# Retention attention with a two-of-eight router and experts: states per head, outputs on four quarter arrays, routed rows in threes, noise loaded later

## The chip, the cores and the metric

The kernel runs on one core of one Trainium2 chip. The metric is the device time of one execution in microseconds (us). A run is called slow when it is more than 1.5% above the fastest run of the same kernel; ratios use fast runs only. On one core a single run's state can't be known, so the two runs that were taken once are called "unknown" below.

The profile names the engines PE (TensorE's matmuls), PEld (its weight loads), DVE (VectorE), ACT (ScalarE), POOL (GpSimd) and SP (SyncE). A name with q behind it, such as SPq, is the part of an engine that issues DMAs.

## The reference

Attention without softmax, with a decay per head, then a noisy router that sends each row to two of eight experts:

```python
# q, k, v: (8 batches, 8 heads, 576 rows, 64); N = 4608 rows, D = 512, E = 8 experts, F = 1024
scores = (1 / sqrt(64)) * q @ k.transpose(0, 1, 3, 2)
gamma  = 1 - 2.0 ** (-5 - arange(8))
Dmat   = where(rel >= 0, gamma[:, None, None] ** rel, 0)          # rel = row - column
x      = ((scores * Dmat) @ v) -> (4608, 512)
noisy  = x @ w_gate + log1p(exp(x @ w_noise)) * noise
top2   = the two largest of noisy; weights = softmax over the two
out[row] += weight * (relu(x[row] @ w1[e]) @ w2[e])               # for both experts of the row
```

## The kernel before

The attention works in 16 units of one batch and four heads. A unit takes its 512 rows as four blocks of 128: it makes scores S within a block, a running state T (keys times values) for what lies before the block, and the output x from both. Units come in four groups of four; when a group is done, its two batches (nine columns of 128 rows) are routed while the next group is computed. The routed rows go to a buffer `xd` in DRAM, from which the experts gather them.

The states, once for each pair of heads (hp), full 128 by 128 products of which only the two diagonal blocks are kept:

```python
def states(self, u, hp):
    p = self.ps.tile([P, 4, P], F32, name="T", bufs=1)
    for c in range(2):
        for k, n in ((P, slice(2 * c + 1, 4)), (HD, slice(2 * c, 2 * c + 1))):
            for r in range(2):
                m = d["vn"][:k, r, c, hs, :]...to_broadcast([k, n.stop - n.start, P])
                nc.tensor.matmul(p[:, n, :], lhsT=d["kn"][:k, r, c, hs, :]..., rhs=m, ...)
    for h in range(2):
        s = slice(h * HD, (h + 1) * HD)
        nc.scalar.activation(T[s, :, s], p[s, :, s], Act.Copy)
```

The output, once for each half e of a block; q is a row half of the array, s a column half:

```python
def out(self, u, e):
    p = self.ps.tile([P, 2, 2, P], F32, name="x", bufs=2)
    q = slice(e * HD, (e + 1) * HD)
    for hp in range(2):
        for c in range(2):
            for r in range(2):
                for h in range(2):
                    nc.tensor.matmul(p[s, hp, c, :], lhsT=d["vn"][q, r, c, 2 * hp + h, :], rhs=d["S", hp, h][q, c, r, :], ...)
    ...  # three more matmuls of 128 by 128 per hp with the states, then VectorE's eviction to xT
```

The router's noise, loaded at the start by ScalarE's queue, and the storing of the routed rows, after all else of a route, one column of 128 rows at a time:

```python
self.rows = ctx.enter_context(tc.tile_pool(name="rtx", bufs=3))
...
for j in range(2):
    for c in range(4):
        nc.scalar.dma_start(out=self.noise[j * HD:(j + 1) * HD, :, c, :], in_=nq[:, j, :, c, :])
    nc.scalar.dma_start(out=self.noiset[j * HD:(j + 1) * HD], in_=nt[:, j])
...
for c in range(C):                                   # C = 9
    pt = ps.tile([P, DM], BF16, name="tr", bufs=2)
    ...                                              # four transposes
    xr = self.rows.tile([P, XW], F32, name="xr")
    nc.scalar.activation(xr[:, :DM // 2].bitcast(BF16), pt, Act.Copy)
    nc.gpsimd.tensor_copy(xr[:, DM // 2:], pl[:, c, :])
    nc.sync.dma_start(out=self.xd[(c0 + c) * P:(c0 + c + 1) * P, :], in_=xr)
    yield
```

A route is a generator: between two parts of a unit the loop runs it on to its next `yield`. So the number of `yield`s says over how many places of the attention a route is spread.

Of the kernel before, what the change touches and what calls it, by code (L numbers as in the profile page):

```python
# [16 lines left out]
P = 128  # L17
N = 4608
NCOL = N // P
E = 8  # L20
# [68 lines left out]
def decay_tables(nc, cp, tmp):  # L89
# [4 lines left out]
    tv = tmp.tile([P, 576], F32, name="tv")  # L94
# [21 lines left out]
class Attention:  # L116


    def __init__(self, tc, ctx, K, q, k, v):
# [11 lines left out]
        self.Tb = [self.cp.tile([P, 4, P], BF16, name=f"Tb{j}") for j in range(8)]  # L131
# [54 lines left out]
    def cast_tail(self, bp):  # L186
        nc = self.nc
        d = {}
        for n in "qk":
            t = self.bf.tile([P, DM], BF16, name=n + "t")  # L190
# [55 lines left out]
    def states(self, u, hp):  # L246
# [4 lines left out]
        p = self.ps.tile([P, 4, P], F32, name="T", bufs=1)  # L251
        hs = slice(2 * hp, 2 * hp + 2)
        first = True
        for c in range(2):

            for k, n in ((P, slice(2 * c + 1, 4)), (HD, slice(2 * c, 2 * c + 1))):
                for r in range(2):
                    m = d["vn"][:k, r, c, hs, :].rearrange("p h d -> p (h d)").unsqueeze(1).to_broadcast(
                        [k, n.stop - n.start, P])
                    nc.tensor.matmul(p[:, n, :], lhsT=d["kn"][:k, r, c, hs, :].rearrange("p h d -> p (h d)"), rhs=m,  # L260
                                     start=first, stop=(c == 1 and k == HD and r == 1), skip_group_check=True)
                    first = False
        T = self.Tb[(2 * u + hp) % 8]
        for h in range(2):
            s = slice(h * HD, (h + 1) * HD)
            nc.scalar.activation(T[s, :, s], p[s, :, s], Act.Copy)  # L266
        d["T", hp] = self.T[bp, b, 2 * hq + hp] = T

    def out(self, u, e):

        nc = self.nc
        d = self.u[u]
# [3 lines left out]
        p = self.ps.tile([P, 2, 2, P], F32, name="x", bufs=2)  # L276
        q = slice(e * HD, (e + 1) * HD)
        for hp in range(2):
            for c in range(2):
                for r in range(2):  # L280
                    for h in range(2):
                        s = slice(h * HD, (h + 1) * HD)
                        nc.tensor.matmul(p[s, hp, c, :], lhsT=d["vn"][q, r, c, 2 * hp + h, :],  # L283
                                         rhs=d["S", hp, h][q, c, r, :], start=(hp == 0 and c == 0 and r == 0),
                                         stop=False, skip_group_check=True)
        for hp in range(2):
            for c in range(2):
                j = 2 * c + e
                if j:
                    nc.tensor.matmul(p[:, hp, c, :].rearrange("p (r q) -> p r q", r=2), lhsT=d["T", hp][:, j - 1, :],  # L290
                                     rhs=d["Q"][:, hp, c, :, e, :], start=False, stop=(hp == 1 and c == 1),
                                     skip_group_check=True)
        xv = self.xT[bp][:, 2 * hq:2 * hq + 2, 4 * b:4 * b + 4, :].rearrange("p y (c e) t -> p y c e t", e=2)[:, :, :, e, :]
        gv = self.gt[:, 2 * hq:2 * hq + 2, :512].rearrange("p y (c e t) -> p y c e t", c=2, e=2)[:, :, :, e, :]
        nc.vector.tensor_tensor(xv, p, gv, Alu.mult)
        if e:
            del self.u[u]
# [28 lines left out]
class Router:  # L326
    def __init__(self, tc, ctx, K, at, wgn, moe_noise, xd, keep):
# [8 lines left out]
        nm = moe_noise.rearrange("(b s) e -> b s e", b=8)  # L336
        nq = nm[:, :512, :].rearrange("b (c q r) e -> q r b c e", q=HD, r=2)
        nt = nm[:, 512:, :].rearrange("(p b) s e -> s b p e", b=2)
        for j in range(2):
            for c in range(4):  # L340
                nc.scalar.dma_start(out=self.noise[j * HD:(j + 1) * HD, :, c, :], in_=nq[:, j, :, c, :])
            nc.scalar.dma_start(out=self.noiset[j * HD:(j + 1) * HD], in_=nt[:, j])
# [4 lines left out]
    def route(self, bp):  # L347
# [7 lines left out]
        for c in range(C):  # L355
# [3 lines left out]
            if c % 3 == 2:  # L359
                yield  # L360
# [638 lines left out]
```

## Time and profile before

| | before |
|---|---|
| timed, three runs | 698.31, 702.89, 708.54 us |
| profiled execution, span | 630.6 us |
| first scores of unit 0 | 35.05 us |
| first scores of units 5, 9, 13 | 83.40, 153.23, 215.02 us |
| end of the attention | 263.4 us |
| first expert matmul | 310.27 us |

The times of units are the starts of their first group of scores (S) on TensorE. The first expert matmul divides the kernel in two: the change touches only what lies before it.

These are the groups of the page that concern the states, the stored rows and the two matmuls of the experts. The columns are line, engine, operation, operands and count, then busy time in all and mean ns of one, then the idle time just ahead of them and what ended most of it.

```profile
L738 PE MATMUL p<-xgT,w 128*128 128x256 bf16 x1280 | 244.4, 275 | 2.4 <-DVE hT L745 0.3
L757 PE MATMUL po<-w,hT 128*128 128x512 bf16 x600 | 226.5, 381 | 6.3 <-DVE o L788 6.3
...
L260 PE MATMUL T<-vn,kn 64*128 64x128 bf16 (+2 forms) x256 | 51.7, 324 | 8.2 <-ACT Tb L266 8.2
...
L266 ACT ACTIVATE Tb<-T 64x256 bf16<-64x256 f32 x64 | 24.2, 378 | 63.1 <-PE T L260 62.7
...
L513 POOL COPY xr<-pl 128x8 f32<-128x8 f32 x36 | 9.9, 292 | 77.9 <-DMA xd<-xr 62.1
...
L512 ACT ACTIVATE xr<-tr 128x512 bf16<-128x512 bf16 x36 | 20.9, 597 | 37.0 <-DMA xd<-xr 19.9
```

Two things are to be seen. The states are the largest TensorE item of the attention (51.7 us busy), and the two engines that fill row buffers wait 62.1 and 19.9 us for stores of rows. And the experts' matmuls run almost without a gap: 2.4 and 6.3 us idle.

### The profile page before, as it was taken

The numbers are of one execution on the slowest core, as the hardware profiler recorded it, in microseconds if no ns is written. First come the engines' busy times: TensorE is split into PE (matmuls) and PEld (weight loads), VectorE is DVE, ScalarE is ACT, GpSimd is POOL, SyncE is SP. The second block draws the span as 40 slices with busy tenths as digits, with TensorE's granted clock in tenths as the row PEclk, the third lists the DMA queues.
The fourth block names the chain that finished last, engine by engine and source line by source line (L and its number), as shares of the span: only waits on it lengthen the run. The fifth ranks groups of instructions, "written<-read, shape, count | busy, mean of one in ns | idle before, by whom it ended". The sixth has DMA issues, their size and how long they took to land.

```text
span 630.6 us, 11565 instructions
## 1 busy us (share of the span) xinstructions
PE 479.9 (76%) x4329; PEld 329.6 (52%) x4369; DVE 277.4 (44%) x727; ACT 296.5 (47%) x449; POOL 313.3 (50%) x393
## 2 busy tenths in 40 slices
PE   0179985757657966604499999999896999999990
PEld 0155653534435644403366666666674666667660
DVE  0034467622782477384422244443442444444440
ACT  5164552334624540603257575666664666544430
POOL 8504324303512310012670277777777767777773
PEclk9999975565658555856599999999998999999996
DMA  9999855094915100411354676778778489666552
GB/s 196 239 267 290 189 151 118 6 219 146 266 27 102 45 2 1 135 76 63 89 160 161 216 273 211 249 231 259 251 273 278 161 287 331 194 198 213 175 190 88
DMA packets 112251, 110.76 MB, mean 176 GB/s; under 512 B 28802, under 2 KB 84611, under 8 KB 112192
## 3 DMA queue, kind: packets, MB, share of 16 engines
q1 hardware_dynamic: 86080, 76.18, 41.0%
q0 software_dynamic: 19232, 32.87, 19.4%
q10 hardware_dynamic: 6880, 0.93, 1.0%
q8 instruction: 35, 0.57, 0.4%
q14 instruction: 24, 0.20, 0.1%
HBM read 91.21 MB, written 41.83 MB: 211 GB/s over the span
## 4 chain that ended last, share of the span: by engine, by line
PE 57%; DVE 14%; DMA 10%; issue 6%; ACT 4%; POOL 4%; SPq 3%; ACTq 0%; POOLq 0%; DVEq 0%
PE p L738 20%; PE po L757 18%; PE T L260 5%; DMA xd<-xr 3%; PE x L283 3%; DMA prv<-yd,ix 2%; PE pt L722 2%; PE tr L222 2%; SPq L153 2%; PE R L498 2%; DVE olo L482 2%; DVE S L243 1%; DMA out_dram<-o,ix 1%; PE S L238 1%; DMA rawt_q<-in_q_dram 1%
## 5 line engine op out<-in xcount | busy, mean ns | idle before, releaser
L738 PE MATMUL p<-xgT,w 128*128 128x256 bf16 x1280 | 244.4, 275 | 2.4 <-DVE hT L745 0.3
L757 PE MATMUL po<-w,hT 128*128 128x512 bf16 x600 | 226.5, 381 | 6.3 <-DVE o L788 6.3
L738 PEld LDWEIGHTS <-w 128*128 128x128 bf16 x1280 | 126.4, 99 | 89.2 <-issue 8.6
L745 DVE TENSOR_SCALAR hT<-p 128x512 bf16<-128x512 f32 x80 | 55.1, 690 | 149.7 <-PE p L738 148.2
L743 ACT ACTIVATE hT<-p 128x512 bf16<-128x512 f32 x80 | 47.8, 597 | 119.3 <-PE p L738 81.4
L766 POOL DMA_INDIRECT prv<-yd,ix x70 | 71.5, 1022 | 50.5 <-DVE hT L745 27.5
L693 POOL DMA_INDIRECT xg<-xd,xi x80 | 80.7, 1009 | 27.1 <-issue 15.5
L794 POOL DMA_INDIRECT out_dram<-o,ix x70 | 71.1, 1016 | 21.4 <-issue 13.1
L243 DVE TENSOR_TENSOR S<-S,mask 128x512 bf16<-128x512 f32 x64 | 41.1, 683 | 82.2 <-PE S L238 82.2
L757 PEld LDWEIGHTS <-hT 128*128 128x128 bf16 x640 | 62.9, 98 | 8.6
L788 DVE SCALAR_TENSOR_TENSOR o<-po,f,prv 128x512 f32<-128x512 f32 x70 | 50.0, 744 | 23.1 <-DMA prv<-yd,ix 19.9
L260 PE MATMUL T<-vn,kn 64*128 64x128 bf16 (+2 forms) x256 | 51.7, 324 | 8.2 <-ACT Tb L266 8.2
L777 ACT ACTIVATE y<-po,f 128x512 f32<-128x512 f32 x80 | 50.4, 683 | 10.0 <-PE po L757 10.0
L266 ACT ACTIVATE Tb<-T 64x256 bf16<-64x256 f32 x64 | 24.2, 378 | 63.1 <-PE T L260 62.7
L178 POOL TENSOR_TENSOR vn<-raw_v,vg 128x1024 bf16<-128x1024 f32 x16 | 30.4, 1902 | 43.0 <-PE x L283 25.3
L173 POOL TENSOR_SCALAR_AFFINE_SELECT kn<-raw_k 128x512 bf16<-128x512 f32 x32 | 22.1, 716 | 58.5 <-PE T L260 37.5
L513 POOL COPY xr<-pl 128x8 f32<-128x8 f32 x36 | 9.9, 292 | 77.9 <-DMA xd<-xr 62.1
L689 ACT ACTIVATE w<-wst 128x1024 bf16<-128x1024 f32 x48 | 47.8, 1047 | 0.0
L725 ACT ACTIVATE xgT<-pt 128x1024 bf16<-128x1024 bf16 x40 | 40.7, 1017 | 10.0 <-DVE f L707 7.6
L260 PEld LDWEIGHTS <-kn 128*128 128x128 bf16 (+1 forms) x256 | 18.3, 108 | 39.9 <-issue 36.1
L222 PE MATMUL tr<-ident,qb 128*128 128x128 bf16 x128 | 15.9, 300 | 29.6 <-ACT qb L182 29.6
L512 ACT ACTIVATE xr<-tr 128x512 bf16<-128x512 bf16 x36 | 20.9, 597 | 37.0 <-DMA xd<-xr 19.9
(167 smaller groups left out, 553.4 us busy)
## 6 DMA issues: line engine op xcount, KB each, us to landing
wst<-in_moe_w_dram SPq DMA_DIRECT2D x48, 512.0 KB, 5.8
yd<-y SPq DMA_DIRECT2D x35, 512.0 KB, 3.7
raw_k<-in_k_dram SPq DMA_DIRECT2D x32, 256.0 KB, 5.7
raw_v<-in_v_dram SPq DMA_DIRECT2D x32, 256.0 KB, 5.2
raw_q<-in_q_dram SPq DMA_DIRECT2D x30, 256.0 KB, 5.4
xd<-xr SPq DMA_DIRECT2D x36, 132.0 KB, 1.7
w<-in_moe_w_dram POOLq DMA_DIRECT2D x4, 1024.0 KB
xg<-xd,xi POOLq DMA_INDIRECT x80
```

What stands on the lines that cost most here:

```text
L243: nc.vector.tensor_tensor(S, p[h], self.K["mask"].unsqueeze(1).to_broadcast([P, 2, 2, P]), Alu.mult)
L260: nc.tensor.matmul(p[:, n, :], lhsT=d["kn"][:k, r, c, hs, :].rearrange("p h d -> p (h d)"), rhs=m, start=first, stop=(c == 1 and k == HD a ...
L689: nc.scalar.activation(W[e][:, k * F:(k + 1) * F], t, Act.Copy)
L693: nc.gpsimd.indirect_dma_start(out=xgs[i % NX][:, s, :], out_offset=None, in_=xd[:, :], in_offset=IOff(ap=keep["xi"][:, 2 * i + s:2 * i + ...
L738: nc.tensor.matmul(p1[:, f2, :], lhsT=w[:, o:o + P], rhs=xgT[:, di, :], start=(di == 0), stop=(di == KD - 1))
L743: nc.scalar.activation(hT[:, 2 * fp:2 * fp + 2, :], p1, Act.Relu)
L745: V.tensor_relu(hT[:, 2 * fp:2 * fp + 2, :], p1)
L757: nc.tensor.matmul(po[s], lhsT=hT[:, fi, s * P:(s + 1) * P], rhs=w[:, o:o + DM], start=(fi == 0), stop=(fi == KF - 1))
L766: nc.gpsimd.indirect_dma_start(out=prv[i % NP][:, s, :], out_offset=None, in_=yd[:rows, :], in_offset=IOff(ap=st[i]["ix"][:, s, 1:2], axis=0),
L777: nc.scalar.activation(y[:, s, :], po[s], Act.Copy, scale=g[:, s:s + 1])
L788: V.scalar_tensor_tensor(o[:, s, :], st[i]["po"][s], st[i]["g"][:, s:s + 1], prv[i % NP][:, s, :], Alu.mult, Alu.add)
L794: ins = nc.gpsimd.indirect_dma_start(out=out[:, :], out_offset=IOff(ap=st[i]["ix"][:, s, 0:1], axis=0), in_=st[i]["o"][:, s, :], in_offset ...
```

## The change

Its intent: fewer and shorter steps for TensorE in a unit (states only for the blocks that are kept, outputs on all four quarters of the array), no wait for stores of rows (three buffers of three columns, filled early in the route), and a start that does not stand behind the noise. The diff, cut to its core:

```diff
-    def states(self, u, hp):
+    def states(self, u):
-        p = self.ps.tile([P, 4, P], F32, name="T", bufs=1)
+        p = self.ps.tile([P, 2, 4, HD], F32, name="T", bufs=1)
         for c in range(2):
             for k, n in ((P, slice(2 * c + 1, 4)), (HD, slice(2 * c, 2 * c + 1))):
                 for r in range(2):
-                    m = d["vn"][:k, r, c, hs, :]...to_broadcast([k, n.stop - n.start, P])
-                    nc.tensor.matmul(p[:, n, :], lhsT=d["kn"][:k, r, c, hs, :]..., rhs=m, ...)
+                    for hp in range(2):
+                        for h in range(2):
+                            m = d["vn"][:k, r, c, 2 * hp + h, :]...to_broadcast([k, n.stop - n.start, HD])
+                            nc.tensor.matmul(p[h * HD:(h + 1) * HD, hp, n, :], lhsT=d["kn"][:k, r, c, 2 * hp + h, :], rhs=m, ...)
         for h in range(2):
-            nc.scalar.activation(T[s, :, s], p[s, :, s], Act.Copy)
+            nc.scalar.activation(T[s, :, :, s]..., p[s]..., Act.Copy)
[...]
-    def out(self, u, e):
+    def out(self, u):
-        p = self.ps.tile([P, 2, 2, P], F32, name="x", bufs=2)
+        p = [self.ps.tile([P, 2, 2, P], F32, name="x", bufs=2) for e in range(2)]
         for hp in range(2):
             for c in range(2):
                 for r in range(2):
                     for h in range(2):
-                        nc.tensor.matmul(p[s, hp, c, :], lhsT=d["vn"][q, r, c, 2 * hp + h, :], rhs=d["S", hp, h][q, c, r, :], ...)
+                        for e in range(2):
+                            q = slice(e * HD, (e + 1) * HD)
+                            nc.tensor.matmul(p[e][s, hp, c, :], lhsT=d["vn"][q, r, c, 2 * hp + h, :], rhs=d["S", hp, h][q, c, r, :], ...)
[...]
+    def load_noise(self, j):          # called in units 1 and 2, on SyncE's queue
[...]
     def route(self, bp):
+        xr = [self.rows.tile([P, 3, XW], F32, name="xr") for j in range(3)]
+        def row(c):
+            ...                       # four transposes, then
+            nc.scalar.activation(xr[c // 3][:, c % 3, :DM // 2].bitcast(BF16), pt, Act.Copy)
+        row(0)                        # one row(c) after each of the next steps
[...]
+        for j in range(3):            # ahead of the tables olo and oh
+            nc.gpsimd.tensor_copy(xr[j][:, :, DM // 2:], pl[:, 3 * j:3 * j + 3, :])
+            nc.sync.dma_start(out=self.xd[t0:t0 + 3 * P, :]..., in_=xr[j])
-        for c in range(C):            # the loop of nine single rows at the end
-            ...
[...]
         at.load(0, (nc.scalar, nc.sync, nc.sync))
-        at.load_tail(0, (nc.scalar, nc.sync, nc.sync))
-        for u in (1, 2, 3):
+        at.load(1, (nc.scalar, nc.sync, nc.sync))
+        at.load_tail(0, (nc.sync,) * 3)
+        for u in (2, 3):
             at.load(u, (nc.sync,) * 3)
[...]
-        at.cast_tail(0)               # now at the end of unit 0
-        at.tr_tail(0)
```

"Tails" are the last 64 rows of each batch, which don't fill a block. The route's product for the ranks (line 455 after) also moved, behind the computation of the weights.

## The prediction

> **What bounds the kernel now.** I read the busy slices first, to split the span into stages; then the chain of waits in order of time, for what ends last in each; then the timeline of single stretches, for the length of one step.
>
> ```profile
> PE   0179985757657966604499999999896999999990
> DVE  0034467622782477384422244443442444444440
> PEclk9999975565658555856599999999998999999996
> DMA  9999855094915100411354676778778489666552
> ```
>
> One slice is 15.8 us. From slice 20 on (about 310 us) TensorE is nearly full: the experts, which the change does not touch. Before it lie two slices of almost no TensorE work, sixteen units of attention with routing between them, and from 263 to 310 us a trough. No engine is full there, so that part is a chain of waits. The first expert matmul starts at 310.27 us; whatever comes off before it comes off the end. The timed runs (702.89 us) are 70 us longer than the profiled execution (630.6 us of span). Nothing in the page tells where those 70 us lie; I assume that they lie in what stays.
>
> Start, from the timeline:
>
> ```profile
> 16.48 5.38 ACTq L341 DMA_DIRECT2D noise<-in_moe_noise_dram  x4
> 22.30 0.60 ACTq L342 DMA_DIRECT2D noiset<-in_moe_noise_dram  x1
> 22.94 4.40 ACTq L341 DMA_DIRECT2D noise<-in_moe_noise_dram  x4
> 28.45 1.06 ACT L182 ACTIVATE qb<-raw_q 128x1024 bf16<-128x1024 f32 x1 [15.30 <-DMA noise<-in_moe_noise_dram]
> ```
>
> ScalarE's own queue issues ten noise loads before it may cast the first q: 15.30 us idle, though both casts of k were over at 13.6 us. Unit 0 starts its scores at 35.1 us.
>
> A unit without routing, TensorE's timeline:
>
> ```profile
> 42.99 0.64 PE L238 MATMUL S<-QT,KT 64*64 64x128 bf16 x16
> 43.42 1.06 PE L283 MATMUL x<-S,vn 64*64 64x128 bf16 x16
> 44.42 0.39 PE L290 MATMUL x<-QT,Tb 128*128 128x128 bf16 x2
> ...
> 48.27 1.83 PE L260 MATMUL T<-vn,kn 128*128 128x384 bf16 x8
> 51.01 1.78 PE L260 MATMUL T<-vn,kn 128*128 128x384 bf16 x8 [0.92 <-ACT Tb L266]
> 52.72 0.64 PE L238 MATMUL S<-QT,KT 64*64 64x128 bf16 x16
> ```
>
> From S to S is one unit: 9.73 us. TensorE sets it; only the second T waits, for the eviction of the first out of the one T buffer. The same 16 matmuls of 64x64 by 128 columns take 0.43 us as S and 1.00 us as x (start to next start).
>
> A unit in which routed rows are stored, and the last route:
>
> ```profile
> 144.33 0.60 ACT L512 ACTIVATE xr<-tr 128x512 bf16<-128x512 bf16 x1 [9.24 <-DMA xd<-xr]
> 144.98 1.01 PE L222 MATMUL tr<-ident,kn 128*128 128x128 bf16 x8 [7.59 <-ACT xr L512]
> ```
>
> ```profile
> 282.62 2.46 DVE olo L482
> ...
> 289.04 2.58 PE R L498 x18
> 292.13 0.61 ACT xr L512
> 292.79 2.09 DMA xd<-xr
> ...
> 299.53 1.71 DMA xd<-xr
> 301.31 0.59 issue
> ```
>
> Three row buffers for nine rows: ScalarE waits for a store that stands in SyncE's queue behind loads, and TensorE waits for ScalarE. At the end the nine rows follow each other by themselves, after the last table is finished.
>
> **What the Trainium skill says.** "TensorE: Matmul & The Clock Gate", Part 3 (packing small matmuls): tiles of the array at different row and column positions run at once. The trace agrees: S alternates over four quarters, 27 ns a matmul; x keeps one row half and alternates two columns, 62 ns. The same page, Part 1, has a cold clock at half rate, 107 ns for 128 columns. The trace agrees in durations (8 transposes from 47.42 to 48.27 us, 106 ns each; 68 ns each from 78.04 to 78.58), though the granted clock in the page reads 9 in both. "TensorEngine Tiling (Array Packing)", Key Properties: a change of tiling mode drains the engine. The T group streams 2 x 384 + 6 x 128 columns, 1.28 us at the cold rate, and took 1.63 to 1.83, so four changes of shape may cost 0.35 us or more. "DMA: Bandwidth & Descriptors", Specifications, wants 512 bytes or more for line rate; the noise lies in pieces of 32 bytes, and its queue (q10) took 1.0% of 16 engines' span, 6.3 us, for 0.93 MB including two q loads. Agreed.
>
> **The change part by part.**
>
> *Start.* The noise goes to SyncE during units 1 and 2, unit 1 is loaded before the tails, the tail casts come after unit 0. ScalarE ends its tables at 13.1 us and can cast q then, if q has landed (loads here took 5 to 8 us). Cast 1.06, transposes 1.05, two evictions of 1.02, less overlap: scores at about 17.5 us instead of 35.1. Gain 17.6 us.
>
> *Outputs.* 32 matmuls go from 2.00 us to 32 x 27 ns = 0.87 us: 1.1 us a unit cold, 0.5 us warm.
>
> *States.* Two heads' full product, of which half was thrown away, becomes one column half per head: 8 matmuls of 192 columns and 24 of 64, run in pairs. Four pairs of 160 ns plus 12 pairs of 60 to 110 ns plus drains of 0.4 us: 2.1 us, instead of 48.27 to 52.72 = 4.45 us. Gain 2.3 us, of which 0.9 is the wait for the T buffer. ScalarE: two evictions of 512 columns at about 0.6 us (its row of 512 columns took 597 ns) for four of 378 ns, 0.3 us less.
>
> *A unit without routing:* 9.7 - 1.1 - 2.3 = 6.3 us. DMA is near: the loads run full up to 65 us, 16.2 MB in 65 us, 250 GB/s; a unit with its share of tails is 1.7 MB or 6.7 us, and the noise now adds 6 us in between. So I take 17.5 us + 4.5 (unit 0) + four steps of about 7 + 2 for tails and noise: step 5 begins at 52 us instead of 83.4. Gain 31 us, the start included.
>
> *Routing.* The steps that lay on the path go: TensorE no longer waits for the cumulated counts (2.00 us at 96.90) since that product comes after the weights; three buffers of three rows, filled during the route, replace three of one row. VectorE's work stays: per four units 16 S of 683 ns, 8 xT of 688 ns, tails about 3 us, and the route, about 15 us (150.0 us busy before 304 us, less S, xT, tails and memsets, over 4), together 34 to 37 us. By the order of VectorE's instructions the route now falls into the first three steps of each four. Step 5: about 11.8 us of VectorE; step 6: 15.2 (olo 2.5, oh 1.65 twice); steps 7 and 8 are TensorE's, 8.7 (with 18 table matmuls) and 7.6. Sum 43 us, 45 with some blocking. Before, the groups took 70 us (83.4 to 153.2), 62 us (to 215.0) and 48 us (to 263.4, its last step without a new unit). After: 45, 45 and 40. Gains 25, 17 and 8: 50 us. The attention would end at 52 + 130 = 182 us.
>
> *End.* From 263.4 to 292.4 us (the list of rows) VectorE's chain is kept; it includes 7 us of memsets. The gather began at 302.13 us because of the rows' stores; with the rows stored under olo and oh it can begin about 0.5 us after the list. Gain 9 us. Gather to first expert matmul, 8 us, stays.
>
> *Sum.* 17.6 + 13.8 (31.4 in all up to step 5) + 50 + 9 = 90 us. The profiled span becomes about 540 us; the timed median 702.9 - 90 = 613 us. I write 615.
>
> **The rivals.**
>
> *DMA becomes the bound.* Faster units demand loads faster. Sixteen units at 6.7 us, noise 6 us, four halves of expert weights of about 7 us each, stores of two routes about 4.5 us each: 150 us until unit 15 has landed. Step 14 wants it; by my sum the middle of step 14 is at about 161 us. So it only just does not bind. For it: DMA share above 1 up to 65 us. Against: it was idle at 105 to 125 and 180 to 195 us. If it bound by 20 us, 635 us.
>
> *VectorE takes the whole gain of the states.* The route is packed into fewer steps, its olo and oh stand in front of evictions of S, and TensorE waits there. For it: TensorE already waited 20.9 us for oh and 12.7 us elsewhere for VectorE's copies. Against: two whole steps of each four are free of routing. If the groups took 55, 55 and 45 us, 640 us.
>
> *Outputs and states gain nothing* because small matmuls are bound by their issue. Against: S shows 27 ns a matmul, 17 ns when warm. Then units stay at 9.7 us and only start, rows and end remain, about 45 to 50 us: 655 us.
>
> *Better than the sum:* a TensorE with fewer gaps runs warm more often (a unit at about 4 us instead of 6.3), and the 70 us of the timed runs may lie partly in the part that shrinks: 590 us.
>
> **Range and chances.** Three rivals cost 20 to 40 us and hardly all at once; one gains 25. 80% range 588 to 648 us. Even the start and the end alone, 27 us, are 3.8% of 703, and neither depends on another engine's speed beyond loads that have landed. Faster by over 2%: 0.96; within 2%: 0.03; slower: 0.01.
>
> **What would show it.** The first S at about 17 us (if q lands late, it shows as a wait on q's load). A unit of 6 to 7 us between 25 and 50 us; x on four quarters at 27 ns or less a matmul, T as one group of about 2 us without a wait in it. No wait of ScalarE on the stores of rows. S evictions late behind olo and oh in step 6. The attention's end at about 182 us, the first gather right after the list, the first expert matmul at about 220 us and 320 us of experts after it. The prediction would be wrong if the noise loads, now on SyncE in front of the loads of units 5 and 6, starved TensorE there; if 64-column states took as long as before; or if the expert stage itself became longer.

## The result, and the profile after

The changed kernel is correct and takes 628.92 us (median of four runs, 620.63 to 632.7); the kernel before took 703.41 us in the median of the four runs beside it (698.31 to 708.54). The ratio is 0.8902, with a 95% interval from 0.8785 to 0.9019: faster. A ratio here is the mean time of one kernel's fast runs over the mean of the other's fast runs of the same rounds, so it is not quite the quotient of the two medians. The profiled execution of the changed kernel spans 626.8 us.

The busy slices of the changed kernel, 15.7 us each, in tenths:

```profile
PE   0688668558763246999889889699699779889980
...
DVE  0366886896887741222334334144144224323440
...
PEclk9977657658656558899979889789889979969996
DMA  9997999996023222447646647457667764554542
```

Counted from 0, the trough before the experts now lies at slices 12 to 14, where the kernel before had it at 17 to 19. But from slice 16 on the experts show digits of 6 and 7 every few slices, which the kernel before did not show in its profile.

Two units before routing starts, TensorE's timeline of the changed kernel (start, length, engine, line, operation, then in brackets an idle time and what ended it):

```profile
28.26 0.64 PE L238 MATMUL S<-QT,KT 64*64 64x128 bf16 x16
28.68 1.07 PE L285 MATMUL x<-S,vn 64*64 64x128 bf16 x32
29.68 0.82 PE L293 MATMUL x<-QT,Tb 128*128 128x128 bf16 x6
30.30 1.06 PE L222 MATMUL tr<-ident,qb 128*128 128x128 bf16 x8
31.29 0.64 PE L238 MATMUL S<-QT,KT 64*64 64x128 bf16 x16
31.86 1.04 PE L222 MATMUL tr<-ident,kn 128*128 128x128 bf16 x8
32.83 1.25 PE L259 MATMUL T<-vn,kn 128*64 128x192 bf16 x32
34.33 0.42 PE L238 MATMUL S<-QT,KT 64*64 64x128 bf16 x16 [0.25 <-ACT KT L225]
```

From S to S it is 6.07 us, where the kernel before took 9.73. All 32 output matmuls take 1.00 us (28.68 to 29.68), as long as 16 of them took before; the states are one group of 1.25 us with nothing to wait for inside. (TensorE works at two rates in these traces: eight transposes of 128 columns in a row start about 107 ns apart at one and 56 ns apart at the other. "Cold clock" and "warm clock" below mean these two. The states and the S after them ran on the warm clock, so not all of the 3.66 us is the change.)

The unit ahead of it went less well. It starts at 17.34 us, and then TensorE stands still for the tails:

```profile
20.96 1.91 PE L259 MATMUL T<-vn,kn 128*64 128x192 bf16 x32
24.96 0.29 PE L209 MATMUL tr<-ident,qt 128*128 128x128 bf16 x1 [2.10 <-ACT qt L193]
27.40 0.29 PE L209 MATMUL tr<-ident,kt 128*128 128x128 bf16 x1 [2.15 <-POOL kt L195]
```

The end of the last route in the changed kernel:

```profile
217.45 2.56 PE L524 MATMUL R<-oh,olo 128*128 128x160 bf16 x18 [7.95 <-DVE oh L518]
...
220.79 0.24 DVE L540 SCALAR_TENSOR_TENSOR xi<-xrow,z 128x80 int32<-128x80 f32 x1
221.89 1.15 POOL L708 DMA_INDIRECT xg<-xd,xi  x1 [6.63 <-DVE cT L555]
```

The list of rows (`xi`) is written at 221.0 us and the first gather starts at 221.9; before, the list was there at 292.6 and the gather began at 302.1.

ScalarE's filling of the row buffers, whose wait for stores was 19.9 us, now waits mostly for TensorE's transposes. From the page after:

```profile
L367 ACT ACTIVATE xr<-tr 128x512 bf16<-128x512 bf16 x36 | 20.7, 595 | 15.8 <-PE tr L366 11.5
```

And the experts' two groups of matmuls, after:

```profile
L753 PE MATMUL p<-xgT,w 128*128 128x256 bf16 x1280 | 261.9, 286 | 26.3 <-issue 23.4
L772 PE MATMUL po<-w,hT 128*128 128x512 bf16 x640 | 253.7, 400 | 19.1 <-issue 14.6
```

They stood idle for 26.3 and 19.1 us, mostly for "issue": the profile shows nothing they waited for. The experts took 395.8 us (231.0 to 626.8) against 320.3 us in the profile of before. So the first expert matmul came 79.3 us earlier, the profiled execution became only 3.8 us shorter, and the timed runs 74.5 us shorter. Taken at its word, the pair of profiles would say that the change saved 79 us and lost 75 of them in the experts. The timed runs contradict that, which is what the first experiment settles.

### The profile page after: what moved, and what is told of

It reads as the page before. It is cut to its first block, busy times and chain, and to the rows that moved or that the text cites. A ratio compares the mean times of both kernels' runs of the same rounds, so it can differ in the third digit from the quotient of the medians.

```text
span 626.8 us, 11951 instructions
## 1 busy us (share of the span) xinstructions
PE 472.1 (75%) x4625; PEld 317.9 (51%) x4625; DVE 282.9 (45%) x727; ACT 291.9 (47%) x417; POOL 318.1 (51%) x365
## 4 chain that ended last, share of the span: by engine, by line
PE 59%; DVE 17%; issue 11%; DMA 4%; ACT 4%; SPq 2%; POOL 1%; another core or an unknown queue 1%; ACTq 0%; POOLq 0%; DVEq 0%
PE p L753 25%; PE po L772 23%; DVE S L243 3%; PE pt L737 2%; PE T L259 2%; DMA raw_q<-in_q_dram 2%; PE R L524 2%; DVE olo L508 2%; DVE xT L299 1%; PE tr L222 1%; DMA xg<-xd,xi 1%; DVE oh L516 1%; DVE oh L513 1%; PE S L238 1%
## 5 line engine op out<-in xcount | busy, mean ns | idle before, releaser
L753 PE MATMUL p<-xgT,w 128*128 128x256 bf16 x1280 | 261.9, 286 | 26.3 <-issue 23.4
L772 PE MATMUL po<-w,hT 128*128 128x512 bf16 x640 | 253.7, 400 | 19.1 <-issue 14.6
L753 PEld LDWEIGHTS <-w 128*128 128x128 bf16 x1280 | 129.9, 102 | 134.6 <-issue 61.1
L772 PEld LDWEIGHTS <-hT 128*128 128x128 bf16 x640 | 64.7, 101 | 33.3 <-issue 23.4
L792 ACT ACTIVATE y<-po,f 128x512 f32<-128x512 f32 x80 | 51.7, 685 | 34.8 <-remote 17.7
L243 DVE TENSOR_TENSOR S<-S,mask 128x512 bf16<-128x512 f32 x64 | 41.1, 683 | 37.7 <-PE S L238 37.7
L704 ACT ACTIVATE w<-wst 128x1024 bf16<-128x1024 f32 x48 | 47.9, 1049 | 0.0
L427 POOL TENSOR_TENSOR cum<-cum,M 128x8 bf16<-128x8 bf16 x36 | 7.2, 199 | 64.5 <-DVE d L432 62.0
L173 POOL TENSOR_SCALAR_AFFINE_SELECT kn<-raw_k 128x512 bf16<-128x512 f32 x32 | 24.0, 775 | 26.4 <-DMA raw_k<-in_k_dram 14.1
L265 ACT ACTIVATE Tb<-T 64x512 bf16<-64x512 f32 x32 | 18.8, 589 | 35.6 <-PE T L259 33.5
L737 PE MATMUL pt<-ident,xg 128*128 128x128 bf16 x320 | 26.5, 225 | 9.4 <-DMA xg<-xd,xi 7.0
L737 PEld LDWEIGHTS <-xg 128*128 128x128 bf16 x320 | 22.0, 100 | 11.8 <-DMA xg<-xd,xi 8.6
L222 PE MATMUL tr<-ident,qb 128*128 128x128 bf16 x128 | 13.7, 272 | 17.4 <-ACT qb L182 14.6
```

Of the source, the lines that this page charges most:

```text
L243: nc.vector.tensor_tensor(S, p[h], self.K["mask"].unsqueeze(1).to_broadcast([P, 2, 2, P]), Alu.mult)
L704: nc.scalar.activation(W[e][:, k * F:(k + 1) * F], t, Act.Copy)
L737: nc.tensor.transpose(pt[:, di, s * P:(s + 1) * P], xb[:, di * P:(di + 1) * P], K["ident"])
L753: nc.tensor.matmul(p1[:, f2, :], lhsT=w[:, o:o + P], rhs=xgT[:, di, :], start=(di == 0), stop=(di == KD - 1))
L772: nc.tensor.matmul(po[s], lhsT=hT[:, fi, s * P:(s + 1) * P], rhs=w[:, o:o + DM], start=(fi == 0), stop=(fi == KF - 1))
L792: nc.scalar.activation(y[:, s, :], po[s], Act.Copy, scale=g[:, s:s + 1])
```

## The experiments

All kernels but one give correct results. The table has, for each profile, the first scores of units 0, 5, 9, 13 and 15, the first expert matmul, and the rest of the span, which is the experts. All in us.

| run | unit 0 | 5 | 9 | 13 | 15 | first expert matmul | experts |
|---|---|---|---|---|---|---|---|
| before | 35.0 | 83.4 | 153.2 | 215.0 | 242.3 | 310.3 | 320.3 |
| before, again | 34.8 | 83.2 | 151.8 | 211.4 | 237.0 | 304.3 | 398.3 |
| changed | 17.3 | 56.1 | 104.0 | 152.2 | 180.6 | 231.0 | 395.8 |
| outputs by halves | 17.3 | 55.7 | 104.6 | 152.7 | 181.5 | 231.0 | 393.2 |
| old states | 17.4 | 65.2 | 121.9 | 178.9 | 210.0 | 261.6 | 397.0 |
| old start | 34.0 | 65.4 | 113.3 | 161.1 | 189.5 | 239.1 | 399.9 |
| late single rows | 17.4 | 57.4 | 123.9 | 178.2 | 204.3 | 267.3 | 401.9 |
| old route | 17.3 | 55.9 | 116.0 | 169.6 | 195.2 | 270.6 | 401.3 |
| tables made once | 17.4 | 56.3 | 103.9 | 148.7 | 174.4 | 223.8 | 396.3 |
| memsets on GpSimd | 17.4 | 56.3 | 104.0 | 151.5 | 179.9 | 224.4 | 398.6 |
| late rows in threes | 17.3 | 54.3 | 105.8 | 159.0 | 185.1 | 243.7 | 397.8 |
| tables spread | 17.3 | 56.0 | 105.6 | 155.7 | 182.0 | 236.8 | 399.9 |
| tail loads later | 17.4 | 57.0 | 105.4 | 153.6 | 181.8 | 232.6 | 402.2 |
| best | 17.3 | 54.1 | 98.8 | 148.4 | 177.2 | 218.3 | 403.3 |

One caution for reading it: the same code may differ by 4 to 6 us from one profile to the next. The last row has the changed kernel's attention, and is at unit 9 at 98.8 against 104.0 us; the two profiles of the kernel before have their first expert matmul at 310.3 and 304.3 us. Each row is one profile, so differences of a few us in this table show nothing by themselves.

### The kernel before, once more

No edit; one more profile of the kernel before.

> The kernel before, unchanged. Its timed runs took 703 us and its profile 631 us, of which the experts (from the first expert matmul at 310 us) took 320 us without gaps; the changed kernel's experts took 396 us in its profile, with TensorE idle in bursts for nothing that the profile shows. Theory: the profile of before fell into a rarer state of the expert stage; a new profile shows the first expert matmul at 310 us again, within 3 us, and about 390 us after it. Rival: the 70 us lie in attention and routing, which the profile flattered; then the first expert matmul comes near 380 us and 320 us follow.

It took 704.15 us, span 702.6, and its first expert matmul stands at 304.3 us. Its experts took 398.3 us and look like those of the changed kernel:

```profile
L738 PE MATMUL p<-xgT,w 128*128 128x256 bf16 x1280 | 260.4, 287 | 25.5 <-issue 21.1
L757 PE MATMUL po<-w,hT 128*128 128x512 bf16 x640 | 253.4, 400 | 23.8 <-issue 19.2
```

So the first profile of before caught a rare execution in which the experts ran almost without gaps. In all 13 other profiles the experts took 393 to 403 us, whichever kernel it was. The change therefore did not slow the experts, and the 70 us by which the timed runs exceed the first profile lie in the experts, as the prediction had assumed. Profile against typical profile, the change gains 73.3 us before the experts (304.3 to 231.0), which agrees with 74.5 us timed.

Where the experts lose the time can be seen in part. Counting each 32 of the first expert product's matmuls as one tile of rows, most tiles take 7.4 us from start to start in every profile, and some take 10 to 20 us: in the changed kernel the tiles 1, 9, 12, 14, 18, 23, 28 and 33 took 18.4, 15.1, 11.4, 13.0, 18.4, 17.1, 18.6 and 18.8 us, and inside them single matmuls of one accumulation start 0.5 to 2 us apart with no semaphore between them. Counted at 10 us and over, 7 to 16 of the 39 tile-to-tile times are long in these 13 profiles. They are not scattered by chance: tiles 1, 9 and 23 are long in all 13, and in the first profile of before only tile 23 is (14.6 us), so the places go with the program, though not what is lost there. I looked for a cause in the fetches of instructions (DMA queues 8 and 14). Some lie inside the long stretches of the changed kernel (at 445.8 us in the one from 444.9 to 456.3) and some of these stretches have none (239.9 to 251.3 us), so they don't explain it. What makes the tiles long was not settled.

### Outputs by halves

```diff
-        for hp in range(2):
-            for c in range(2):
-                for r in range(2):
-                    for h in range(2):
-                        for e in range(2):
+        for e in range(2):
+            for hp in range(2):
+                for c in range(2):
+                    for r in range(2):
+                        for h in range(2):
                             nc.tensor.matmul(p[e][s, hp, c, :], ...)
```

> The changed kernel, but the 32 output matmuls of a unit issued row half by row half again, so that two quarters run at a time. Theory: 32 of them take 2.0 us instead of 1.0 us at the cold rate (0.55 us more when warm), 16 units, TensorE bounds only the steps without routing: first expert matmul 6 to 14 us later than 231 us, time 1 to 2% longer. Rival (VectorE or transfers bound every step): less than 3 us.

It took 629.96 us, ratio 0.9002 (0.8947 to 0.9057), and the first expert matmul came at 231.01 us where the changed kernel has 231.00. My theory fell and the rival held: interleaving all four quarters is worth nothing on the path that these runs can show. The group itself did get longer, on the cold clock and the warm one:

```profile
29.12 1.50 PE L285 MATMUL x<-S,vn 64*64 64x128 bf16 x32
...
42.23 0.87 PE L285 MATMUL x<-S,vn 64*64 64x128 bf16 x32
```

against 1.07 and 0.62 us after the change. That is less than expected. The trace's single matmuls show two chains of eight pairs, the second of which begins at 29.55 us, when three pairs of the first have still to start (29.65 to 29.87 us). The trace doesn't name the row halves; I take the chains for them. The 0.25 to 0.43 us that remain, 4 to 7 us over 16 units, don't appear at the first expert matmul; either other engines end last in those units, or they are lost in the 4 to 6 us by which profiles differ. This run keeps both halves in one call, as the change has it; the older form with two calls at two places of the unit was not run by itself.

### Old states

```diff
-        p = self.ps.tile([P, 2, 4, HD], F32, name="T", bufs=1)      # one group of 32, per head
-        ...
+        for hp in range(2):                                          # two groups of 8, as before
+            p = self.ps.tile([P, 4, P], F32, name="T", bufs=1)
+            ...
+            for h in range(2):
+                nc.scalar.activation(T[s, hp, :, s], p[s, :, s], Act.Copy)
```

> The changed kernel with the states of before: full 128x128 products, two per unit through one T buffer, four evictions. Theory: a unit that TensorE bounds gets 2.3 to 3 us longer, a step that VectorE bounds less; over 16 units first expert matmul 20 to 35 us later, time 3 to 6% longer. Rival (hidden behind VectorE and loads): under 8 us.

It took 661.07 us, ratio 0.9418 (0.9358 to 0.9478); the first expert matmul moved by 30.6 us, to 261.6. The theory holds. Between units 5 and 9 it lost 56.7 - 47.9 = 8.8 us, and between 9 and 13 57.0 - 48.2 = 8.8 us: 2.2 us a unit in both. The lines show the wait that the change removed, here on the warm clock (the narrower products and the missing wait were not parted by a run):

```profile
42.16 1.15 PE L261 MATMUL T<-vn,kn 128*128 128x384 bf16 x8
44.22 1.13 PE L261 MATMUL T<-vn,kn 128*128 128x384 bf16 x8 [0.91 <-ACT Tb L267]
45.28 0.25 PE L319 MATMUL x<-St,vt 128*64 128x128 bf16 x2
```

### Old start

```diff
-        at.load(1, (nc.scalar, nc.sync, nc.sync))
-        at.load_tail(0, (nc.sync,) * 3)
-        for u in (2, 3):
+        at.load_tail(0, (nc.scalar, nc.sync, nc.sync))
+        for u in (1, 2, 3):
             at.load(u, (nc.sync,) * 3)
         ...
+        rt.load_noise(0)              # on ScalarE's queue again
+        rt.load_noise(1)
         ...
+        at.cast_tail(0)
+        at.tr_tail(0)
```

> The changed kernel with the start of before: noise loaded by ScalarE's queue at once, tails before unit 1 and cast before unit 0. Theory: first S near 35 us instead of 17.3; since the first units of the changed kernel wait for loads (unit 1 began at 28.3 us), the late start is partly caught up: first expert matmul 8 to 14 us later. Rival of my own prediction: the whole 17.6 us come back.

It took 640.09 us, ratio 0.9101 (0.9052 to 0.9149). Unit 0 starts 16.7 us later, unit 5 is 9.3 us later, and the first expert matmul 8.1 us; the median is 11.2 us higher. So a start that is 17 us earlier is worth half of that, or somewhat more. With the noise in front unit 0 takes 5.2 us (34.0 to 39.2) and not 10.9: the loads of units 1 to 3 have more time, and the tails are cast and transposed before unit 0 and not at its end. GpSimd's timeline of the changed kernel shows what holds the tails there:

```profile
23.04 1.27 POOL L173 TENSOR_SCALAR_AFFINE_SELECT kn<-raw_k 128x512 bf16<-128x512 f32 x2 [4.66 <-DMA raw_k<-in_k_dram]
24.88 1.90 POOL L178 TENSOR_TENSOR vn<-raw_v,vg 128x1024 bf16<-128x1024 f32 x1 [0.57 <-DMA raw_v<-in_v_dram]
26.73 0.61 POOL L195 TENSOR_SCALAR_AFFINE_SELECT kt<-rawt_k 128x512 bf16<-128x512 f32 x1
```

The cast of the tail's keys (`kt`) stands behind the casts of unit 2, and those wait for the loads of unit 2, though the tail's loads were issued before them (9.5 to 15.1 us against 15.1 to 20.2).

### Late single rows, and late rows in threes

Two runs that part two things which the change did together. The first puts the rows back behind the tables, with single-row buffers:

```diff
-        xr = [self.rows.tile([P, 3, XW], F32, name="xr") for j in range(3)]
-        row(0) ... row(8)             # within the route
-        for j in range(3): ...        # three copies and stores, ahead of the tables
+        for c in range(C):            # behind the tables, as before
+            ...
+            xr = self.rows.tile([P, XW], F32, name="xr")
+            ...
+            nc.sync.dma_start(out=self.xd[(c0 + c) * P:(c0 + c + 1) * P, :], in_=xr)
+            yield
```

> The changed kernel, but the nine rows of a route are transposed, copied and stored one at a time after its last table, through three buffers of one row, as before; the order of the rest of the route stays. Theory: at the end 8 to 9 us come back, and each of three routes inside the attention stalls again on the store of rows (19.9 us of ScalarE's waits in the kernel before): first expert matmul 15 to 25 us later than 231 us, time 2 to 4% longer. Rival (the stalls came from the old late position of SyncE's loads only): 9 us, from the end alone.

It took 670.44 us, ratio 0.9473 (0.9413 to 0.9534): 41 us above the changed kernel, and the first expert matmul 36.3 us later. That is more than the 15 to 25 us that I expected. The second run keeps the late place but the three buffers of three rows:

```diff
+        for c in range(C):            # behind the tables
+            row(c)
+            if c % 3 == 2:
+                nc.gpsimd.tensor_copy(xr[j][:, :, DM // 2:], pl[:, 3 * j:3 * j + 3, :])
+                nc.sync.dma_start(out=self.xd[t0:t0 + 3 * P, :]..., in_=xr[j])
+            yield
```

> The changed kernel with its nine rows of a route moved behind the tables again, as in the run with late rows, but keeping three buffers of three rows and one store per three rows. The late rows with single-row buffers cost about 36 us of the part before the experts (first expert matmul at 267.3 against 231.0 us). Theory A: the single-row buffers cost it, since each row waits for a store that stands behind loads in SyncE's queue; then most comes back here, first expert matmul at 235 to 247 us and 633 to 645 us timed, ratio to the kernel before 0.90 to 0.917. Theory B: the place behind the tables costs it; then the first expert matmul stays at 257 to 267 us and the time at 655 to 670 us, ratio 0.93 to 0.953.

It took 643.57 us, ratio 0.9122 (0.9068 to 0.9176), with the first expert matmul at 243.7 us. Theory A holds: of the 36.3 us, 23.5 (267.3 - 243.7) are the single-row buffers, and 12.7 (243.7 - 231.0) the place. The chain of waits of the run with single rows, cut to its longest pieces (start, length, what), shows how a row buffer costs so much:

```profile
94.70 12.05 DMA raw_v<-in_v_dram
...
114.33 3.19 DMA xd<-xr
...
117.63 0.04 ACT xr L516
...
118.12 0.79 ACT qb L182
...
119.07 1.02 ACT KT L225
```

Between the first two of these, from 106.8 to 114.2 us, SyncE issues loads, one after the other; the store of a row stands behind them in the same queue. ScalarE's cast of q and its eviction of the transposed keys stand behind a filling of a row buffer (L516), and start only after that store has freed one at 117.5 us. So too few row buffers make the attention wait for the loads of units that are four ahead.

### Old route

```diff
-    def route(self, bp):              # the changed one
+    def route(self, bp):              # the whole routine of the kernel before
```

> The changed kernel with the whole route of before: rows late and one at a time, counts' product before the weights, 32 pieces spread over the steps instead of 18. Theory: from 304.3 us (before, second profile) to 231.0 us the change took 73.3 us; states 30.6 and start 8.1 by the first runs, outputs nothing, so the route should be worth the rest, 30 to 38 us. Rival (the parts overlap, and undoing one undoes another's gain): under 25 us, and no more than rows late alone.

It took 673.95 us, ratio 0.9544 (0.9485 to 0.9602); the first expert matmul stands at 270.6 us, 39.6 us later, a little above the 30 to 38 us expected. Against the run with late single rows that is only 3.3 us more. So nearly all that the new route is worth are its rows; that the product for the ranks moved is worth little. One flaw: this route has 32 places, and four faster units offer 28, so each route runs on into the next group and the last into the tail. The late single rows fit exactly (28 places), so, unless two effects cancel, the flaw can only touch those 3.3 us.

### Tables made once

This kernel is wrong on purpose: routes 1 and 2 use the tables of route 0 and make none.

```diff
+        if bp in (1, 2):
+            olo, oh = self.tabs
+            for _ in range(4):
+                yield
+        else:
             olo = ...                 # one comparison of 2304 columns
             oh = ...                  # three operations of 1440 columns
```

> Wrong result on purpose: routes 1 and 2 reuse the one-hot tables of route 0 instead of making them on VectorE (olo, oh and two products of oh, 6.4 us of VectorE each); TensorE multiplies them as before. Theory (VectorE sets the first two steps of each four): the steps that hold them, 18 and 19.7 us, fall to 11 to 13; first expert matmul 9 to 13 us earlier. Rival 1 (TensorE or ScalarE just behind): 2 to 6 us. Rival 2 (loads bound it): under 2 us.

It took 621.91 us (one run), and the first expert matmul came at 223.8 us, 7.2 us earlier and not 9 to 13. The tables of a route are 2.55 + 1.65 + 1.65 + 0.60 = 6.4 us of VectorE where nothing disturbs them, 12.9 us for two routes. Taken at its word, somewhat over half of VectorE's table work sets the end, and the rest hides in the units' slack. This is one profile and one time, so 7.2 us is not far outside the 4 to 6 us by which profiles differ.

### Tables spread

If the tables hurt because they stand in front of evictions of S in the second unit after a route's start, spreading them should help:

```diff
+        for _ in range(2):
+            yield
         olo = ...
-        yield
+        for _ in range(3):
+            yield
         oh = ...
-        yield
+        for _ in range(3):
+            yield
         V.tensor_tensor(oh[:, :, :, 1, :], ...)
```

> The changed kernel with six empty steps put between the routed rows' stores, the table olo and the two halves of the table oh, so that VectorE makes them in the third and fourth unit after a route's start and not all in the second. Theory A: the second unit (18.0 us where 15.2 were predicted) is long because olo and oh stand in front of evictions of S there; spread, each group of four units loses 3 to 5 us, the first expert matmul comes at 216 to 223 us instead of 231.0, and the time is 614 to 621 us, ratio to the kernel before 0.872 to 0.882. Theory B: VectorE's whole work in a group sets its length wherever it stands; then the second unit gets shorter and the third longer, and the first expert matmul stays within 3 us of 231, the time within 625 to 633 us.

It took 637.84 us, ratio 0.9018 (0.8958 to 0.9077). Neither theory had that: it is slower. All four runs (633.3 to 639.5 us) lie above those of the changed kernel (up to 632.7), though the two intervals of the ratios overlap. Units 5 to 9 took 49.6 us against 47.9, so within a group nothing was won. At the end the loss is plain. The tables of the third group's route now fall so late that the end of the attention waits for them:

```profile
182.42 2.46 DVE olo L510
...
187.28 1.56 DVE oh L516
...
190.04 1.58 DVE oh L520
...
191.65 0.61 DVE oh L522
```

This is from the chain of waits of the run with spread tables. In the changed kernel the same four operations lie between 174.6 and 183.2 us, most of them in unit 14; here they end at 192.3 us, the attention's last matmul starts at 197.8 us against 191.7, and nothing is left to hide them behind. Spreading work evenly is worth nothing when it pushes work past the last place where it could hide.

### Memsets on GpSimd

In the last route VectorE also zeroes the experts' buffers, between 192.6 and 203.2 us.

```diff
-            nc.vector.memset(xgs[j], 0.0)
+            nc.gpsimd.memset(xgs[j], 0.0)
...
-            nc.vector.memset(prv[j], 0.0)
+            nc.gpsimd.memset(prv[j], 0.0)
```

> The changed kernel with the experts' eleven memsets moved from VectorE to GpSimd, which is idle at the end of routing. Theory: they stand in VectorE's chain of the last route between 192.6 and 203.2 us, 7.1 us of it; first expert matmul 5 to 7 us earlier, time 0.8 to 1.1% shorter. Rival (GpSimd's memsets delay the counts, which it makes, or hold VectorE's port): no gain.

The first expert matmul came at 224.4 us, 6.6 us earlier, as expected; from the first scores of unit 15 it is 44.5 us and not 50.4. The time is 625.96 us, ratio 0.885 (0.8796 to 0.8904). The interval overlaps that of the changed kernel, so the gain is seen in the profile and not shown by the times.

### Tail loads later

```diff
-        at.load_tail(0, (nc.sync,) * 3)
-        for u in (2, 3):
-            at.load(u, (nc.sync,) * 3)
+        at.load(2, (nc.sync,) * 3)
+        at.load_tail(0, (nc.sync,) * 3)    # cast and transposed at the end of unit 1
+        at.load(3, (nc.sync,) * 3)
-        nc.sync.dma_start(out=yd[:P, :], in_=zero)   # at the start; now in unit 6
```

> The changed kernel with the loads of the first tails moved behind those of unit 2 (cast and transposed one unit later), and the store of zeros moved from the start to unit 6. Theory A: unit 0 takes 10.9 us instead of the predicted 4.5 since the loads of units 1 and 2 come late behind other transfers at a full DMA; with 1 MB out of the way unit 2 starts 2 to 4 us earlier (34.3 before), step 5 at 52 to 54 instead of 56.1 us, and the first expert matmul 2 to 4 us earlier, 227 to 229 us; the time 625 to 628 us. Theory B: the transfers are only moved, and whatever is won up to unit 2 is lost again by unit 5: step 5 within 1 us of 56.1, and the first expert matmul within 1.5 us of 231.

It took 632.08 us, ratio 0.895 (0.8898 to 0.9003). Unit 1 now starts at 22.5 us where it was 28.3, but unit 2 starts at 34.8 against 34.3, and unit 5 at 57.0 against 56.1. Theory B holds, but for 0.1 us (it allowed 1.5 at the first expert matmul, which is 1.6 later). The wait is the same one unit later:

```profile
26.03 1.25 PE L259 MATMUL T<-vn,kn 128*64 128x192 bf16 x32
31.52 0.29 PE L209 MATMUL tr<-ident,qt 128*128 128x128 bf16 x1 [4.25 <-ACT qt L193]
33.92 0.29 PE L209 MATMUL tr<-ident,kt 128*128 128x128 bf16 x1 [2.11 <-POOL kt L195]
```

The DMA engines are full in both (shares of 1.15 to 1.29 between 17 and 34 us), so it may be that the bytes set the pace here. But one rival is left: the tail's casts still stand behind those of the unit two ahead, which is now unit 3 (GpSimd casts its keys and values from 29.63 us on, after 7.11 us of waiting for the load, and `kt` at 33.25 us). The run moved the loads and not that order, and an earlier place for the tail's casts was not tried.

### A version with the memsets moved and the second tile transposed later

The first expert matmul waits for four gathers, since the transposes of the second tile of rows stand in front of it.

```diff
             transp(0)()
-            transp(1)()
...
-            for _ in g1(0, {}):
+            for _ in g1(0, {1: lambda: transp(1)()}):
                 pass
```

together with the memsets on GpSimd.

> The changed kernel with the memsets of the experts' buffers on GpSimd, as in the run before that was 6.6 us earlier at the first expert matmul (224.4 us), and with the transposes of the second tile put into the middle of the first tile's matmuls, so that those need two gathers and not four. Theory A: the first tile's activations are complete at about 222.0 us there, so the first expert matmul comes at 221 to 223 us, the time falls with it to 617 to 625 us, ratio to the kernel before 0.875 to 0.884. Theory B: the first two tiles took 23 to 25 us together in every profile but the first of before, whatever stood ahead of them, so the 2.4 us are lost there again: first expert matmul at 221 to 223 us all the same, but a time within 2 us of the run with the memsets alone (626 us, ratio 0.885).

The first expert matmul came at 218.3 us, of which 3.4 us are a shorter tail (41.1 us from unit 15) and the rest a lucky attention (unit 15 at 177.2). The time is 624.82 us, ratio 0.8851 (0.8801 to 0.8901), the same as with the memsets alone. Theory B holds for the time (the first expert matmul came still earlier than its 221 us): the first two tiles took 12.0 + 14.0 us, and the experts 403.3 us, the longest of all. This version beats the kernel before, and its median is 4 us below the changed kernel's, but that difference is within the intervals.

## Why the prediction was right or wrong

The time was predicted as 615 us, range 588 to 648; 628.9 us is inside, and "faster by over 2%" is right. The gain was 74.5 us and not 88. Before the experts the sum had 31.4 us up to unit 5, 50 in the groups and 9 at the end; against the same profile they measured 27.3, 44.3 and 7.6, 79.3 in all. The second profile of before has 6.0 us less to lose there, hence 73.3. Step by step:

- **What bounds it.** Right. The part before the experts shrank from 304 or 310 to 231 us and the experts did not change. The assumption about the 70 us was right and is now shown. It was an assumption on one profile, though: the 320 us of experts predicted for the profiled execution were the exception.
- **Start, 17.6 us.** The first S was predicted at 17.5 and came at 17.3. But the sum counted this gain in full, and that is the step that failed: the term "4.5 (unit 0)" measured 10.9 us, tails included (for tails and noise the sum had 2 more), so unit 5 began at 56.1 and not at 52 us. The next four steps took 27.8 us, as the sum had them (28). Putting the old start back costs 8.1 us, not 17.6. The rival "DMA becomes the bound" was right in part in the first 35 us, where I had not looked for it: units waited for loads there. At unit 14, where I had, no wait for a load stands in the chain of waits, though the DMA engines were full up to about 145 us. Moving the tail's loads did not help; how much of the 10.9 us are bytes, and how much the order of the casts, stays open.
- **Outputs, 1.1 us a unit.** The group took 1.00 us for 32, near the 0.87 predicted, but undoing the four-quarter order lengthened it by only 0.43 us (cold) and left the first expert matmul where it was. This term of the sum is zero on the path as far as it was undone and as far as one profile shows.
- **States, 2.3 us a unit.** Right: 2.2 us a unit measured, 30.6 us in all. The group took 1.25 us on the warm clock (1.91 in unit 0, on the cold one) and not 2.1, which made up for the outputs: a unit came out at 6.07 us where 6.3 was predicted, by errors that cancel.
- **Routing, groups of 45, 45 and 40 us.** 47.9, 48.2 and 39.5 us measured. In the first group the four units took 12.2, 18.0, 9.65 and 8.0 us where 11.8, 15.2, 8.7 and 7.6 were predicted. The second is the term that was mis-sized. A table of that unit in each of the three groups, with the busy time of PE, PEld, DVE, ACT and POOL and the number of instructions, then the clock, DMA share and GB/s, shows VectorE as its bound:

```profile
68.30:86.30 18.00, 9.98 (x143) 7.66 (x142) 17.38 (x45) 6.16 (x10) 11.24 (x13) 0.50 1.10 223
...
116.20:135.90 19.70, 10.07 (x147) 7.69 (x150) 19.09 (x45) 6.28 (x10) 11.71 (x13) 0.50 1.04 261
...
164.40:180.60 16.20, 9.40 (x147) 7.03 (x147) 15.04 (x44) 5.26 (x9) 5.47 (x6) 0.61 0.16 55
```

  VectorE is busy for 17.38 of 18.00 us and for 19.09 of 19.70. In the third group, where GpSimd has no units left to cast (5.47 us busy and not 11), it does nearly the same work in 15.04 us. Why it takes longer beside GpSimd is seen in single durations. VectorE's timeline of the changed kernel has:

```profile
69.22 1.85 DVE L442 TENSOR_TENSOR df<-df,low 128x9 f32<-128x9 f32 x1
...
83.85 2.50 DVE L513 TENSOR_TENSOR oh<-iota,hib 128x1440 bf16<-128x1440 bf16 x1
```

  and GpSimd's at the same times:

```profile
69.15 1.90 POOL L178 TENSOR_TENSOR vn<-raw_v,vg 128x1024 bf16<-128x1024 f32 x1
...
83.80 1.03 POOL L199 TENSOR_TENSOR vt<-rawt_v,vgt 128x512 bf16<-128x512 f32 x1
```

  The operation on 9 columns took 0.17 us in all four routes of the kernel before; here it ends when GpSimd's multiplication does (71.05 us). The first operation of `oh` took 1.65 us everywhere in the kernel before and 2.50 here: it waits out GpSimd's 1.03 us. Six short operations between 67.9 and 73.0 us and the three of `oh` took together 5.2 us more than the same ones undisturbed (0.50 + 0.41 + 1.68 + 0.48 + 0.46 + 0.52 + 0.85 + 0.05 + 0.27); in the kernel before a single one of them, at 1.86 us, was hit. The difference, 3.5 us, is near the 2.8 us missing. The Trainium skill, page "SBUF — State Buffer", section "Who interferes with whom", says that a VectorE instruction with two inputs in SBUF and a GpSimd instruction that reads SBUF exclude each other, and so does one with a single input (as lines 450 and 518 have) when it runs in a two-port mode. The durations agree. I did not move GpSimd's casts away in an experiment, so the size of this term is read from the trace and not shown by a run. My sum took each VectorE duration from a kernel in which GpSimd happened to work at other times.
- **Rows.** The prediction named the wait but gave the rows no number of their own. They are most of the new route's worth: 36.3 of 39.6 us.
- **End, 9 us.** From the attention's end to the first expert matmul it took 46.9 us before and 39.3 after, so 7.6 us. The wait that was meant, from the list to the first gather, fell from 9.5 to 0.9 us; the way from there to the first expert matmul grew from 8.1 to 9.1.
- **Rivals.** That VectorE takes the whole gain of the states was wrong, and so was that small matmuls are bound by their issue. "Better than the sum" was wrong.

The parts undone one at a time cost 8.1 (start), 0 (order of outputs), 30.6 (states) and 39.6 us (route) before the experts, 78.3 in all, and the two profiles of before stand 79.3 and 73.3 us from the changed kernel. So, as far as single profiles tell, the parts add up before the experts, and no large gain or loss is hidden between them there. The timed medians add up less well: 11.2, 1.0, 32.2 and 45.0 us, 89.4 in all against 74.5. Some of that is the experts, which took up to 5.5 us longer in these profiles than in the changed kernel's; the rest is not explained.

## What to carry to other kernels

Take a second profile of the kernel before trusting where its time lies: one of two here had a stage 78 us shorter than usual, and a comparison with it would have invented a loss. An earlier start is worth only what the loads behind it, and the casts that wait for them, allow; compare what has landed with what is needed for the first few units. And a store that frees a buffer should not stand behind bulk loads in the same queue when an engine's next work stands behind the wait for that buffer: here it was worth 23 us to bundle the stores and give them nine rows of room.

## What the Trainium skill lacked or had wrong

- "TensorE: Matmul & The Clock Gate" (Part 3) and "TensorEngine Tiling (Array Packing)" (Key Properties): they say that tiles at different positions run at once. The first also says that weight loads for other rows of the array are pulled ahead, and that the matmuls themselves are not reordered. With the two row halves given one after the other, 32 matmuls took 1.43 us cold and 0.80 us warm, against 1.00 and 0.56 us interleaved, and the starts show two chains that overlap by four pairs. If the chains are the two row halves in the kernel's order, which the trace does not name, matmuls did pass each other here.
- "TensorEngine Tiling (Array Packing)" (Key Properties): it says that a change of mode drains the engine, without a size. Here the first 128x128 matmul after the 64x64 outputs started 0.24 us after the last of them cold and 0.15 us warm, where pairs of outputs start 0.11 and 0.06 us apart.
- "SBUF — State Buffer" (Who interferes with whom): agrees. A size for small operations would help: one of 9 columns took 1.85 us instead of 0.17 beside a GpSimd multiplication of 1.90 us.
- No page has it: 7 to 16 of the experts' 39 tile-to-tile times were 10 to 20 us instead of 7.4, with matmuls of one accumulation 0.5 to 2 us apart and no wait shown; the experts took 393 to 403 us in 13 profiles of 14, and 320 us in one.
